# Theta and token mixing of the first three units as whole fp32 products, with their weights split afterwards

## The chip, the cores and the metric

One core of a Trainium2 chip runs one kernel with one launch. The metric is device time in microseconds (us). The engines are called here by their profile names or in words: PE (TensorE, products), PEld (its weight loads), DVE (VectorE), ACT (ScalarE), POOL (GpSimd) and SP (which issues every copy of this kernel). The kernel before takes 648.9 us, the median of three runs (648.49 to 651.3).

## What is computed

Three layers run one after another on 4 sequences of 768 tokens with 384 channels. The attention is a recurrence with a decay per channel; the second layer turns each channel by an angle, mixes over tokens with two 768x768 matrices and then over channels; the third is a gated layer. The change lies in the second layer.

```python
# attention, per head:  state = alpha_t * state + k_t v_t^T ;  y_t = q_t . state
theta = x @ w_theta
zr, zi = x * cos(theta), x * sin(theta)
y = einsum('ts,bsd->btd', w_tok_r, zr) + einsum('ts,bsd->btd', w_tok_i, zi)
u = x + y
x2 = u + maximum(u @ w_ch, 0)
h = maximum(x2 @ w_in, 0)
u3, v = h[..., :512], h[..., 512:]
v_s = einsum('ts,bsd->btd', w_spatial, layernorm(v)) + b_spatial
out = (u3 * v_s) @ w_out
```

The weights w_theta, w_tok_r, w_tok_i, w_ch, w_in and w_out arrive as 64-bit floats. The rest is fp32.

## The kernel before, in words

**Units.** A unit `u` is 128 tokens of one sequence. There are 24, six to a sequence (a "batch", `b`). For each unit the attention runs first (lines 442 to 556: two scans on DVE, `kh` and `qh`, scores `psa`, state `psu`, output `psy`). Then come theta and the mixing: a transposition `pst` (line 568), copies `xh` and `xT` of it, theta (`th_p`, lines 591 and 594), rounding and sine (`kk`, `r`, `z`), `z` times `x` (line 620), and the token mixing `tokmix` (line 652), which adds this unit's six products (three groups of 128 channels, real and imaginary) into five accumulators `acc` of its batch. After a batch's sixth unit the accumulators are added to `xT` (`evac`, line 666), one is cleared for the next batch (`acc_zero`, line 661), and the channel mixing `ch_p` (line 689) follows. The third layer (lines 763 to 870) runs after all units.

**Products in three.** A theta or mixing product is made of reduced fp32 (fp32r) operands. Each operand is held as a high part, which is the rounded value, and a low part, which is what the rounding left. High times high, high times low and low times high are added. For theta that is nine products of 384 columns a unit (six at line 591, three at line 594). For one mixing step it is six instructions, three of 512 and three of 256 columns. The attention products are whole fp32 instead: one instruction in the code, shown as two records in the trace.

**Weights.** A weight piece is 128 rows of 384 numbers. `conv` (line 370) issues ten or so steps for one: a copy of the 64-bit words into one of two buffers `raw` (line 313), `sgn` and `sign` on ACT (lines 319 and 341; for one piece in four the first is on DVE, line 321), `bits` and `join` on DVE (lines 329 and 336), `mag` on ACT (line 344), the product with the sign `mul` (line 349), the high part `high` on ACT (line 355, or 357 for theta) and the low part `low` (line 364, or 366 for theta). The first 30 pieces are three of w_theta, four for each unit of a batch from the two mixing matrices, and three of w_ch; they are all wanted while the first batch runs. GpSimd does `mul` of every third piece (`MULP`), `low` of two in four (`LOP`), and the low part of `z` (`z_l`, line 629) of the first six units (`ZLP`).

**Order.** A planner (`order` and `latest`, lines 86 and 195) lists all steps by due time, moved by a table of offsets per kind of step (`OFF`, and `OFF0`, `OFF3` for the first and last batch), and the instructions are issued in that list's order. Every engine works through its own instructions strictly in it. PSUM has three shared buffers (`psp`), beside the accumulators.

Of the kernel before, what the change touches and what calls it, by code (L numbers as in the profile page):

```python
# [218 lines left out]
def attention_mixer_kernel(  # L219
# [131 lines left out]
    def high(n):
        c = cvs[n]
        f = c["f"].rearrange("p (a b) -> p a b", a=c["a"])
        if c["scale"] is None:
            nc.scalar.copy(out=c["part"](0), in_=f)  # L355
        else:
            nc.scalar.activation(c["part"](0), f, AF.Identity, scale=c["scale"])

    def low(n):
        c = cvs[n]  # L360
        f = c["f"].rearrange("p (a b) -> p a b", a=c["a"])
# [1 line left out]
        if c["scale"] is None:
            c["eng"].tensor_tensor(out=c["part"](1), in0=f, in1=h, op=ALU.subtract)  # L364
        else:
            nc.vector.scalar_tensor_tensor(
                out=c["part"](1), in0=f, scalar=c["scale"], in1=h, op0=ALU.mult, op1=ALU.subtract
            )

    def conv(src, part, key, tiles=(), scale=None):  # L370
# [8 lines left out]
        if src.dtype == I64:  # L379
            k0 = step(OFF["raw"], "dma", 1.6, raw_f64, n, after=before, tiles=[raw, *tiles])  # L380
            raws.append(k0)
            k1 = step(OFF["sgn"], *(("act", 0.54) if n % 4 < SGA else ("dve*", 0.27)), sgn, n, after=[k0], tiles=[raw, sg])
            k2 = step(OFF["bits"], "dve*", 0.27, bits, n, after=[k0], tiles=[raw, cv])
            k2 = step(OFF["bits"], "dve*", 0.47, join, n, after=[k2], tiles=[raw, cv])
            k3 = step(OFF["sgn"], "act", 0.52, sign, n, after=[k1], tiles=[sg])
# [743 lines left out]
```

## Time and profile before

| | before |
|---|---|
| median of 3 runs | 648.9 us |
| the profiled execution | 648.46 us, of which its span in the trace is 646.7 us |
| PE busy | 600.4 us (93%) |
| DVE busy | 431.3 us (67%) |
| ACT busy | 283.4 us (44%) |
| POOL busy | 79.2 us (12%) |

PE is busy nearly all the time, so only two things can change the span: how much work PE has, and how long it stands idle or runs at the slower of its two clock levels. In the page's 40 slices the idle time lies in the first eight (0 to 130 us). DVE is busiest in just these slices, and so is POOL.

### The profile page before, as it was taken

To read this page: it belongs to the slowest core of one execution; us is meant where nothing else is said; L and a number is where in the kernel's file an instruction comes from. 1 tells how busy PE (TensorE), PEld (TensorE's weight loads), DVE (VectorE), ACT (ScalarE), POOL (GpSimd) and SP (SyncE) were. 2 spreads that over 40 slices of the span, in tenths; PEclk is the share of its full clock that TensorE was granted. 3 is DMA by queue.
4 is the path that set the end of the run, shared out by engine and by line. 5 is a ranking of instruction groups with operands and counts; after the bars stand their busy time and mean duration, and the time that the engine had idled before them with its cause. 6 is when DMAs were issued, how large, how long until landed. Compare 5 with 4: busy or idle time off the path is not lost.

```text
span 646.7 us, 13064 instructions
## 1 busy us (share of the span) xinstructions
PE 600.4 (93%) x5364; PEld 560.2 (87%) x5364; DVE 431.3 (67%) x779; ACT 283.4 (44%) x544; POOL 79.2 (12%) x78
## 2 busy tenths in 40 slices
PE   1476697999999999999999999999999999999997
PEld 1465586788888889988888999999999999999997
DVE  6978988799878787777867768684536533563331
ACT  3357677675234353332448744462423331333122
POOL 1023253241000000000001122220100010010000
PEclk9987999999999999999999999999999999999999
DMA  7766644542532243342224464320100010001002
GB/s 200 203 186 185 186 135 135 152 119 61 155 116 74 79 119 98 104 116 77 60 77 133 131 218 144 139 98 1 50 25 0 14 38 25 1 13 50 13 1 73
DMA packets 41147, 61.46 MB, mean 95 GB/s; under 512 B 4864, under 2 KB 30720, under 8 KB 40576
## 3 DMA queue, kind: packets, MB, share of 16 engines
q1 hardware_dynamic: 41088, 60.64, 31.6%
q8 instruction: 42, 0.69, 0.4%
q14 instruction: 17, 0.14, 0.1%
HBM read 47.94 MB, written 9.44 MB: 89 GB/s over the span
## 4 chain that ended last, share of the span: by engine, by line
PE 85%; DMA 5%; DVE 4%; ACT 3%; SPq 1%; issue 1%; POOL 0%; DVEq 0%; ACTq 0%; POOLq 0%
PE acc L652 22%; PE sp L833 15%; PE psv L776 8%; PE pu L818 8%; PE po L862 8%; PE psc L689 6%; PE psy L549 6%; PE th L591 4%; PE psa L482 3%; PE psu L515 2%; DMA raw<-in_w_theta 2%; PE th L594 2%; DMA raw<-in_w_tr 1%; PE psk L499 1%; DMA sd<-ss 1%; PE pst L568 1%
## 5 line engine op out<-in xcount | busy, mean ns | idle before, releaser
L652 PE MATMUL acc<-w,zs 128*128 128x512 f32 (+1 forms) x864 | 174.7, 347 | 0.0
L652 PEld LDWEIGHTS acc<-w,zs 128*128 128x128 f32 x864 | 135.0, 190 | 18.2 <-issue 0.2
L833 PE MATMUL sp<-w,vns 128*128 128x384 f32 x576 | 105.0, 336 | 0.0
L833 PEld LDWEIGHTS sp<-w,vns 128*128 128x128 f32 x576 | 99.9, 188 | 0.0
L849 ACT CAST gs<-t 128x384 fp32r<-128x384 f32 x32 | 16.3, 513 | 99.1 <-DVE t L843 94.4
L818 PE MATMUL pu<-xs,w 128*128 128x384 f32 x288 | 55.7, 337 | 0.0
L776 PE MATMUL psv<-w,xs 128*128 128x256 f32 x432 | 55.5, 283 | 0.0
L842 DVE TENSOR_TENSOR t<-sp,bsb 128x384 f32<-128x384 f32 x32 | 17.8, 557 | 55.5 <-PE sp L833 55.0
L776 PEld LDWEIGHTS psv<-w,xs 128*128 128x128 f32 x432 | 54.5, 191 | 0.2
L862 PE MATMUL po<-w,gs 128*128 128x384 f32 x288 | 53.0, 336 | 0.0
L818 PEld LDWEIGHTS pu<-xs,w 128*128 128x128 f32 x288 | 50.8, 188 | 0.0
L862 PEld LDWEIGHTS po<-w,gs 128*128 128x128 f32 x288 | 49.8, 188 | 0.0
L349 POOL TENSOR_TENSOR wf<-wf,sg 128x384 f32<-128x384 f32 x14 | 17.6, 1259 | 245.9 <-ACT wf L344 244.3
L549 PE MATMUL psy<-sd,qh 112*64 112x96 f32 x352 | 36.7, 262 | 11.8 <-DMA sd<-ss 5.1
L482 PE MATMUL psa<-qh,kh 48*64 48x64 f32 x768 | 30.2, 233 | 17.2 <-DVE kh L463 16.5
L482 PEld LDWEIGHTS psa<-qh,kh 48*64 48x64 f32 x768 | 26.8, 145 | 22.2 <-DVE kh L463 17.0
L689 PE MATMUL psc<-us,wch 128*128 128x256 f32 x324 | 43.3, 284 | 0.0
L689 PEld LDWEIGHTS psc<-us,wch 128*128 128x128 f32 x324 | 40.9, 190 | 0.9
L549 PEld LDWEIGHTS psy<-sd,qh 112*64 112x64 f32 x352 | 24.9, 143 | 17.0 <-issue 7.4
L364 POOL TENSOR_TENSOR w<-wf,w 128x384 fp32r<-128x384 f32 x24 | 28.7, 1198 | 68.8 <-ACT w L355 68.7
L549 PE MATMUL psy<-vd,am 128*64 128x96 f32 x384 | 36.7, 263 | 0.0
L455 DVE TENSOR_TENSOR_SCAN al<-al,heads 112x536 f32<-112x536 f32 x24 | 34.2, 1423 | 0.8
(83 smaller groups left out, 962.3 us busy)
## 6 DMA issues: line engine op xcount, KB each, us to landing
qk<-in_qka SPq DMA_DIRECT2D x24, 448.0 KB, 4.3
al<-in_qka SPq DMA_DIRECT2D x24, 234.5 KB, 3.0
vd<-in_vt SPq DMA_DIRECT2D x48, 96.0 KB, 2.5
raw<-in_w_tr SPq DMA_DIRECT2D x12, 384.0 KB, 4.0
raw<-in_w_ti SPq DMA_DIRECT2D x12, 384.0 KB, 3.7
x2d<-xT SPq DMA_DIRECT2D x12, 384.0 KB, 3.1
x<-x2d SPq DMA_DIRECT2D x4, 1152.0 KB, 5.2
out<-o SPq DMA_DIRECT2D x24, 192.0 KB, 1.9
```

The source lines that it names most:

```text
L364: c["eng"].tensor_tensor(out=c["part"](1), in0=f, in1=h, op=ALU.subtract)
L455: nc.vector.tensor_tensor_scan(out=line, data0=line, data1=one, initial=0.0, op0=ALU.mult, op1=ALU.add)
L482: nc.tensor.matmul(psa[o0:o0 + 64, a, c, :], kh[r0:r0 + D, a, c, :], qh[r0:r0 + D, a, c, :], start=True, stop=True,)
L549: nc.tensor.matmul(psy[64 * c:64 * c + 64, a, :], w[:, a, c, :], v[:, c, :, a, :], start=part == 0 or first, stop=part == 1,)
L591: nc.tensor.matmul(th, xh[:, 0, k], wth[:, pr, k], start=(k == 0 and pr == 0), stop=False)
L652: nc.tensor.matmul(acc[b, n][:, c0:c1], zs[:, pl, ri, m * 128:(m + 1) * 128], w[:, pr, t0:t1], start=first and n != 1, stop=last, skip_gro ...
L689: nc.tensor.matmul(ps, wch[:, pl, k, m * 128:(m + 1) * 128], us[:, pr, k], start=(n == 0), stop=(n == 3 * KD - 1),)
L776: nc.tensor.matmul(ps[:, c], xs2[:, pl, k, o:o + 128], w[:, pr, k], start=(n == 0), stop=(n == 3 * KD - 1),)
L818: nc.tensor.matmul(pu, win[f // 2][:, pl, (f % 2) * KD + k], xq[b, h][:, pr, k], start=(n == 0), stop=(n == 3 * KD - 1),)
L833: nc.tensor.matmul(sp[:, :TH], vns[b, s][:, pl, f * 128:(f + 1) * 128], wsp[s][:, pr, h], start=(n == 0), stop=(n == 3 * NS - 1),)
L842: nc.vector.tensor_tensor(out=t1, in0=s2.pop(("sp", b, f, h))[:, :TH], in1=bsb[0][:, t], op=ALU.add)
L862: nc.tensor.matmul(po, gs[b][:, pl, f, s * 128:(s + 1) * 128], wo[f // 2][:, pr, f % 2], start=(n == 0), stop=(n == 3 * KF - 1),)
```

## The change

For units 0 to 2 theta and the token mixing take the operands whole, in fp32: one product where there were three. `z` of these units is written once and has neither a high nor a low part; `xh` is not made. Their weights (w_theta, and the pieces of both matrices for the first three rows) are kept whole in four extra buffers `wf` out of the twelve of `w`; the high and low parts, which batches 1 to 3 still want, are made after the last product that reads the whole form (`users`, `held`). The scale of w_theta moves into `mag`. `LOP`, `MULP` and `ZLP` are set so that GpSimd gets no `low`, `mul` or `z_l` at all. All offset tables have new numbers, and there are two new ones, per unit in the batch order (`UNIT`, added in `at`) and per weight piece (`PIECE`, added in `conv`).

```diff
-LOP = 2
+LOP = 0
-MULP = 3
-ZLP = 6
+MULP = 99
+ZLP = 0
+FU = 3
...
     def mag(n):
-        nc.scalar.activation(cvs[n]["f"], cvs[n]["f"], AF.Abs)
+        nc.scalar.activation(cvs[n]["f"], cvs[n]["f"], AF.Abs, scale=cvs[n]["scale"])
...
     def mul(n):
         c = cvs[n]
         eng = nc.gpsimd if c["mulp"] else nc.vector
-        eng.tensor_tensor(out=c["f"], in0=c["f"], in1=c["sg"], op=ALU.mult)
+        f = c["f"]
+        if c["users"]:
+            a = c["a"]
+            f, sg = (x.rearrange("p (a b) -> p a b", a=a) for x in (f, c["sg"]))
+            eng.tensor_tensor(out=c["hold"](), in0=f, in1=sg, op=ALU.mult)
+            return
+        eng.tensor_tensor(out=f, in0=f, in1=c["sg"], op=ALU.mult)
+
+    def whole(n):
+        c = cvs[n]
+        return c["hold"]() if c["users"] else c["f"].rearrange("p (a b) -> p a b", a=c["a"])
...
+        nc.scalar.copy(out=cvs[n]["part"](0), in_=whole(n))
...
+        c["eng"].tensor_tensor(out=c["part"](1), in0=whole(n), in1=h, op=ALU.subtract)
...
-        k = step(OFF["high"], "act", 0.41, high, n, after=[k], tiles=[cv, *tiles])
+        k = step(early + OFF["high"], "act", 0.41, high, n, after=[k, *users], tiles=[*(held or [cv]), *tiles])
...
+    def f_tile(key):
+        if key not in wf:
+            wf[key] = wpool.tile([128, 2, S], F32, tag="w", name="wf", bufs=12)
+        return wf[key]
...
     def conv_tok(ri, s):
         src = (w_tr, w_ti)[ri]
         w = w_tile(wt, (ri, s), 1)
+        after = [("low", n) for n in sorted(late)] if (ri, s) == (1, NS - 1) else []
         for h in range(2):
             c = slice(h * TH, (h + 1) * TH)
+            more = {}
+            if s < FU:
+                late.add(len(cvs))
+                more = {
+                    "users": [("tokmix", s, m, ri) for m in range(KD)],
+                    "hold": lambda c=c: f_tile(s)[:, ri, None, c], "held": [("w", 12, ("f", s))],
+                }
...
+    def th_f(u):
+        th = st[u]["th"] = ps_tile([128, DM], "th")
+        for k in range(KD):
+            nc.tensor.matmul(th, xt_ap(u)[:, k], wth_whole()[:, k], start=(k == 0), stop=(k == KD - 1))
...
     def z_m(u):
         z, x = st[u]["z"], st[u]["x"]
-        nc.vector.tensor_tensor(out=z, in0=z, in1=x[:, None, :].to_broadcast([128, 2, DM]), op=ALU.mult)
+        out = z
+        if u < FU:
+            st[u]["zs"] = pb.tile([128, 2, 2, DM], F32, tag="zs", name="zf", bufs=3)
+            out = st[u]["zs"][:, 1]
+        nc.vector.tensor_tensor(out=out, in0=z, in1=x[:, None, :].to_broadcast([128, 2, DM]), op=ALU.mult)
...
-        w = wt[ri, i]
-        for pl, pr in ((0, 0), (0, 1), (1, 0)):
-            first = i == 0 and ri == 0 and pl == 0 and pr == 0
+        whole = u < FU
+        w = wf[i][:, ri, None] if whole else wt[ri, i]
+        for pl, pr in ((1, 0),) if whole else ((0, 0), (0, 1), (1, 0)):
+            first = i == 0 and ri == 0 and (whole or pl == 0 and pr == 0)
...
-            return step(OFF[name] + more.get(name, 0.0), eng, cost, fn, u, *args, after=after, tiles=tiles, by=by)
+            return step(OFF[name] + more.get(name, 0.0) + UNIT.get(str(u), 0.0), eng, cost, fn, u, *args, after=after, tiles=tiles, by=by)
```

What that does to the order is seen at three places. GpSimd, from its start, before; `sd` and `vd` are attention tiles that are cleared, `wf` and `w` a weight piece whole and split, `sg` its sign, `zs` the parts of `z`:

```order
L277 MEMSET sd_96 112x768
L280 MEMSET vd_98 128x768
L277 MEMSET sd_100 112x768
L280 MEMSET vd_102 128x768
L349 ISA
L349 TENSOR_TENSOR wf<-wf,sg 128x384
L364 TENSOR_TENSOR w<-wf,w 128x384
```

and now, the same stretch; the last row is a step of the third layer:

```order
L288 MEMSET sd_96 112x768
L291 MEMSET vd_98 128x768
L288 MEMSET sd_100 112x768
L291 MEMSET vd_102 128x768
L841 ISA
L841 TENSOR_TENSOR rs<-rs,mhalf 128x1 x24
```

All 46 products, low parts of weights and low parts of `z` that stood between the two are gone from it; they stand on DVE now, except the `z` parts of units 0 to 2, which are gone.

PE at the first token mixing, unit 0, before; each of the last two rows stands there three times, in turn, for the three parts:

```order
L568 MATMUL pst<-cst_sb,x 128x128 x3
L499 MATMUL psk<-cst_sb,kh 128x112 x4
L482 MATMUL psa<-qh,kh 64x64 x16
L652 MATMUL acc_109<-w,zs 128x256
L652 MATMUL acc_666<-w,zs 128x512
```

and now:

```order
L584 MATMUL psy<-sd_96,qh 64x96 x2
L584 MATMUL psy<-vd_98,am 64x96 x2
L697 MATMUL acc_109<-wf,zf 128x256
L697 MATMUL acc_533<-wf,zf 128x512
L697 MATMUL acc_549<-wf,zf 128x512
L697 MATMUL acc_550<-wf,zf 128x256
L550 MATMUL psu<-vn,kt 64x48
```

A mixing step is two instructions in place of six, and it stands ahead of the scores `psa` of unit 4 and not behind them.

DVE where batch 0 ends and batch 1's accumulator is cleared, before (`xT` receives the accumulators, `wch` is a piece of w_ch):

```order
L336 SCALAR_TENSOR_TENSOR wf<-raw,wf 128x384
L666 TENSOR_TENSOR xT<-acc_773,xT 128x512
L666 TENSOR_TENSOR xT<-acc_109,xT 128x256
L349 TENSOR_TENSOR wf<-wf,sg 128x384 x2
L666 TENSOR_TENSOR xT<-acc_109,xT 128x256
L666 TENSOR_TENSOR xT<-acc_666,xT 128x512
L364 TENSOR_TENSOR wch<-wf,wch 128x384
L329 TENSOR_SCALAR wf<-raw 128x384
L661 MEMSET acc_1743 128x512
```

and now:

```order
L711 TENSOR_TENSOR xT<-acc_658,xT 128x512
L711 TENSOR_TENSOR xT<-acc_109,xT 128x256
L348 SCALAR_TENSOR_TENSOR wf<-raw,wf 128x384
L379 TENSOR_TENSOR wch<-wf,wch 128x384
L711 TENSOR_TENSOR xT<-acc_109,xT 128x256
L711 TENSOR_TENSOR xT<-acc_533,xT 128x512
L367 TENSOR_TENSOR wf<-wf,sg 128x384
L706 MEMSET acc_1843 128x512
```

The clearing is DVE's instruction 222 before and 267 now.

## Rows read from the trace of the kernel before

**Rows 1.** Busy time by stretch: length; busy us (instructions) by engine; clock; DMA.
```profile
0.00:13.00 13.00, 0.28 (x5) 0.28 (x6) 6.78 (x17) 3.86 (x7) 2.97 (x8) 1.00 0.68 186
13.00:60.00 47.00, 27.94 (x412) 23.86 (x411) 39.16 (x75) 26.03 (x53) 9.25 (x7) 0.88 0.73 197
60.00:126.00 66.00, 55.07 (x549) 48.27 (x550) 56.89 (x100) 44.77 (x91) 25.04 (x16) 0.93 0.53 153
126.00:646.70 520.70, 517.15 (x4406) 487.81 (x4404) 328.53 (x590) 208.72 (x396) 41.94 (x48) 1.00 0.25 76
```

**Rows 2.** The same view, one stretch of PE at its lower clock.
```profile
55.80:62.50 6.70, 5.58 (x44) 4.73 (x45) 5.27 (x12) 4.97 (x10) 3.42 (x3) 0.50 0.69 211
```

**Rows 3.** Waits of DVE, 7 to 126 us: total us, times, longest.
```profile
DVE sg L321 <- DMA raw<-in_w_tr: 6.0, 3, 4.5
...
DVE xh L581 <- ACT xT L577: 3.0, 3, 1.3
```

**Rows 4.** Single lines of DVE, 7 to 126 us: duration ns min/median/max.
```profile
L455 DVE TENSOR_TENSOR_SCAN al<-al,heads x9: 1274/1276/2487, 9.6 to 107.5; 112x536 f32<-112x536 f32 x9
...
L470 DVE TENSOR_TENSOR qh<-qk,al x9: 679/691/2322, 11.4 to 113.1; 112x512 f32<-112x512 f32 x9
...
L329 DVE TENSOR_SCALAR wf<-raw x25: 329/354/1435, 7.2 to 123.9; 128x384 uint32<-128x384 uint32 x25
```

**Rows 5.** Groups of DVE, 7 to 126 us: busy us, mean ns of one, idle before.
```profile
L455 DVE TENSOR_TENSOR_SCAN al<-al,heads 112x536 f32<-112x536 f32 x9 | 14.6, 1625 | 0.3
...
L329 DVE TENSOR_SCALAR wf<-raw 128x384 uint32<-128x384 uint32 x25 | 10.8, 433 | 8.2 <-DMA raw<-in_w_theta 4.9 <-DMA raw<-in_w_ti 2.9 <-DMA raw<-in_w_tr 0.2
L349 DVE TENSOR_TENSOR wf<-wf,sg 128x384 f32<-128x384 f32 x16 | 8.9, 555 | 1.4 <-ACT wf L344 1.4
L470 DVE TENSOR_TENSOR qh<-qk,al 112x512 f32<-112x512 f32 x9 | 8.6, 958 | 1.0 <-PE psy L549 1.0
...
L620 DVE TENSOR_TENSOR z<-z,x 128x768 f32<-128x768 f32 x5 | 4.9, 972 | 0.6 <-ACT z L614 0.6
```

**Rows 6.** Instructions of DVE in order, 90 to 96 us: start, duration.
```profile
90.51 0.68 DVE L489 TENSOR_TENSOR am<-psa,cst_sb 128x512 f32<-128x512 f32 x1
91.11 0.35 DVE L537 TENSOR_TENSOR tmp<-psu,ss 112x192 f32<-112x192 f32 x1
...
91.89 1.27 DVE L451 TENSOR_TENSOR_SCAN rt<-al,heads 112x536 f32<-112x536 f32 x1
...
93.44 2.49 DVE L455 TENSOR_TENSOR_SCAN al<-al,heads 112x536 f32<-112x536 f32 x1
```

**Rows 7.** The same stretch on POOL.
```profile
91.92 2.88 POOL L629 TENSOR_TENSOR zs<-z,zs 128x768 fp32r<-128x768 f32 x1 [0.37 <-DVE ss L524]
```

**Rows 8.** The chain that ended last: start us, us, what.
```profile
7.23 0.65 ACT sg L319
...
157.25 1.08 PE psa L482 x32
...
170.49 1.48 PE psy L549 x32
171.97 0.53 PE psk L499 x4
...
177.81 0.60 PE psu L515 x26
...
182.89 1.05 PE acc L652 x6
```

**Rows 9.** PE in order: `psy` near 195 us.
```profile
195.36 0.33 PE L549 MATMUL psy<-sd,qh 112*64 112x96 f32 x4
195.53 0.34 PE L549 MATMUL psy<-vd,am 128*64 128x96 f32 x4
```

**Rows 10.** PE in order where the first mixing of unit 6 begins.
```profile
146.69 0.49 PE L568 MATMUL pst<-cst_sb,x 128*128 128x128 f32 x3
146.94 1.29 PE L652 MATMUL acc<-w,zs 128*128 128x256 f32 x6
```

More of the change, by code (lines that the diff above doesn't have):

```diff
@@ L43 @@
 OFF = {
[6 rows of a table removed]
-    "sgn": -23.49, "mag": 39.17, "mul": -72.53, "high": -59.59, "low": 17.5, "v": -1.84, "vr": 121.16, "vb": 138.25,
-    "vw": -48.53, "vm": 45.12, "vh": -80.17, "vl": 72.49, "g_u": -21.79, "g_r": -32.74, "g_s": -40.03, "g_m": -104.87,
-    "g_h": -88.37, "g_l": 5.15, "o_p": -6.46, "o_e": 26.76, "x2h": 78.95, "x2l": 23.69, "x2": -32.84,
[6 rows of a table added]
+    "bits": 19.52, "sgn": -39.0, "mag": 43.2, "mul": -77.37, "high": -58.7, "low": 7.1, "v": 9.91, "vr": 13.15,
+    "vb": -3.08, "vw": 17.45, "vm": -5.55, "vh": -54.65, "vl": 17.18, "g_u": -9.94, "g_r": -6.45, "g_s": -45.14,
+    "g_m": -139.46, "g_h": -63.43, "g_l": -44.96, "o_p": 13.88, "o_e": -31.29, "x2h": 130.7, "x2l": 57.91,
+    "x2": -170.04,
 }
@@ L302, in attention_mixer_kernel @@
     conv_done = {}
+    conv_whole = {}
     raws = []
@@ L348, in mul, with conv @@
         eng = nc.gpsimd if c["mulp"] else nc.vector
-        eng.tensor_tensor(out=c["f"], in0=c["f"], in1=c["sg"], op=ALU.mult)
-    def high(n):
[L352 to L357, printed above, removed]
+        f = c["f"]
[8 more added lines that the diff above has]
+        return c["hold"]() if c["users"] else c["f"].rearrange("p (a b) -> p a b", a=c["a"])
+    def high(n):
+        nc.scalar.copy(out=cvs[n]["part"](0), in_=whole(n))
     def low(n):
         c = cvs[n]
-        f = c["f"].rearrange("p (a b) -> p a b", a=c["a"])
         h = c["part"](0).bitcast(F32)
[L363 to L370, printed above, removed]
+        c["eng"].tensor_tensor(out=c["part"](1), in0=whole(n), in1=h, op=ALU.subtract)
+    def conv(src, part, key, tiles=(), scale=1.0, users=(), hold=None, held=(), wait=()):
         n = len(cvs)
-        c = {"src": src, "a": src.shape[1], "part": part, "scale": scale}
+        early = PIECE.get(str(n), 0.0)
+        c = {"src": src, "a": src.shape[1], "part": part, "scale": scale, "users": users, "hold": hold}
         cvs.append(c)
-        pool = scale is None and n % 4 < LOP
+        pool = n % 4 < LOP
         c["eng"] = nc.gpsimd if pool else nc.vector
@@ L379, in conv @@
         if src.dtype == I64:
-            k0 = step(OFF["raw"], "dma", 1.6, raw_f64, n, after=before, tiles=[raw, *tiles])
+            k0 = step(early + OFF["raw"], "dma", 1.6, raw_f64, n, after=before + list(wait), tiles=[raw, *(held or tiles)])
             raws.append(k0)
[L382 to L385, printed above, removed]
+            k1 = step(early + OFF["sgn"], *(("act", 0.54) if n % 4 < SGA else ("dve*", 0.27)), sgn, n, after=[k0], tiles=[raw, sg])
+            k2 = step(early + OFF["bits"], "dve*", 0.27, bits, n, after=[k0], tiles=[raw, cv])
+            k2 = step(early + OFF["bits"], "dve*", 0.47, join, n, after=[k2], tiles=[raw, cv])
+            k3 = step(early + OFF["sgn"], "act", 0.52, sign, n, after=[k1], tiles=[sg])
             c["mulp"] = n % MULP == MULP - 1
-            k2 = step(OFF["mag"], "act", 0.42, mag, n, after=[k2], tiles=[cv])
-            k = step(OFF["mul"], *(("pool*", 0.96) if c["mulp"] else ("dve*", 0.47)), mul, n, after=[k3, k2], tiles=[sg, cv])
+            k2 = step(early + OFF["mag"], "act", 0.42, mag, n, after=[k2], tiles=[cv])
+            k = step(early + OFF["mul"], *(("pool*", 0.96) if c["mulp"] else ("dve*", 0.47)), mul, n, after=[k3, k2], tiles=[sg, cv, *held])
+            conv_whole.setdefault(key, []).append(k)
         else:
-            k = step(OFF["raw"], "dma", 0.8, raw_f32, n, after=before, tiles=[cv, *tiles])
+            k = step(early + OFF["raw"], "dma", 0.8, raw_f32, n, after=before, tiles=[cv, *tiles])
             raws.append(k)
-        k = step(OFF["high"], "act", 0.41, high, n, after=[k], tiles=[cv, *tiles])
-        k = step(OFF["low"], *(("pool*", 0.96) if pool else ("dve*", 0.47)), low, n, after=[k], tiles=[cv, *tiles])
+        k = step(early + OFF["high"], "act", 0.41, high, n, after=[k, *users], tiles=[*(held or [cv]), *tiles])
+        k = step(early + OFF["low"], *(("pool*", 0.96) if pool else ("dve*", 0.47)), low, n, after=[k], tiles=[*(held or [cv]), *tiles])
         conv_done.setdefault(key, []).append(k)
@@ L404, in w_tile, with wth_whole @@
         return part
+    late = set()
+    wf = {}
+    def f_tile(key):
+        if key not in wf:
+            wf[key] = wpool.tile([128, 2, S], F32, tag="w", name="wf", bufs=12)
+        return wf[key]
+    def wth_whole():
+        return f_tile("th").rearrange("p a b -> p (a b)")[:, :KD * DM].rearrange("p (k f) -> p k f", k=KD)
     def conv_tok(ri, s):
@@ L878, in attention_mixer_kernel @@
     step(0.0, "dma", 0.6, load_cst)
-    conv_small(w_theta, wth, "wth", scale=INV_2PI)
+    conv_small(w_theta, wth, "wth", more=lambda k: {
+        "scale": INV_2PI, "users": [("th_f", u) for u in range(FU)],
+        "hold": lambda: wth_whole()[:, k:k + 1], "held": [("w", 12, ("f", "th"))],
+    })
     for s in range(NS):
```

42 lines of the change are left out of this document (26 added, 16 removed), and 36 rows, old and new, of tables (OFF, OFF0, OFF3, PIECE).

## The prediction

> **What bounds the kernel now.** I began with the busy time by stretch [rows 1]. From 126 us on PE is busy 517.2 of 520.7 us at the full clock: there the span is PE's own work. Before that it is not. From 13 to 126 us PE works 83.0 of 113 us, and part of that at the lower of its two levels (granted clock 0.50, 1.2 GHz, [rows 2]). DVE is busy 96.1 of the same 113 us, the most of all engines. Its list in that time holds the attention of eight or nine units and the splitting of 30 weight pieces, so what PE lacks is mostly what DVE has not yet made.
>
> Next, the 17 us that DVE stands idle there. The waits say what for: raw weight copies (6.0 us at line 321, 2.9 and 0.2 at line 329; its 4.9 for w_theta are the start), the copies of the transposed unit on ACT (3.0), the magnitude of a piece on ACT (1.4), PE (1.0) and smaller ones [rows 3, 5].
>
> Last, DVE's busy time is itself longer than its work. A scan of line 455 takes 1.28 us as a rule and 2.49 at worst, a `qh` 0.69 and 2.32, a `bits` 0.35 and 1.44 [rows 4]. The order of time shows when: the scan of 2.49 us stands beside GpSimd's low part of `z`, which began at 91.92 and took 2.88 us [rows 6, 7]. The scan ends (95.9) soon after that low part does (94.8). By means against medians [rows 4, 5] these lines lost 9 x 0.35 + 9 x 0.27 + 25 x 0.08 = 7.6 us; with a few others I put it at 8.5. So GpSimd's help costs DVE part of what it saves.
>
> **A ledger at one point.** To compare the two orders I take one instruction that both have: the first mixing product of unit 6, which opens batch 1. Before, it starts at 146.9 us [rows 10], with 646.7 - 146.9 = 499.8 us of span behind it. It waits for the clearing of the accumulator on DVE, and DVE's part begins with the first raw copy at 7.2 us [rows 8]. So in the new order it starts at 7.2 + (DVE's work ahead of the clearing) + (DVE's waits w), if DVE is what binds.
>
> DVE's work is counted from the order and priced by the distance of neighbours' starts, which is some 0.08 below the duration: `am` 0.68, next start 0.60 later [rows 6]. So 0.27 for the 0.35 instructions, 0.47 for the 0.55 ones, 0.87 for `z`, 0.60 for `kh`, `qh`, `am` [rows 4 to 6], and 2.74 for a unit's two scans with the reciprocal (1.55 to the second scan's start and 1.19 for it undisturbed).
>
> Before: 9 scans 24.7, 27 of 0.60 16.2, 33 state steps 8.9, `bits` and `join` (30 and 29) 21.7, 20 `mul` 9.4, 16 `low` 7.5, 7 signs 1.9, 7 `r` and 8 `xl` 7.1, 7 `z` and one low part 7.0, the first batch's end 2.7: **107.0 us**.
> After: 11 scans 30.1, 33 of 0.60 19.8, 41 state steps 11.1, `bits` and `join` (29 each) 21.5, 29 `mul` 13.6, 28 `low` 13.2, 7 signs 1.9, 8 `r` and 6 `xl` 6.6, 8 `z` and 5 low parts 11.3, end 2.7: **131.7 us**.
>
> Of the 24.7 us more, some 13 come from GpSimd (12 `low`, 9 `mul`, 4 low parts of `z`); the rest is attention of units 9 and 10, brought forward. The two `z` parts and the two `xl` of the first units that vanish are already off.
>
> **What PE has done by then.** The same forward move lies in PE's order: attention of units 9 and 10 stands ahead of the point now, 2 x (1.08 + 0.53 + 0.60 + 1.48), theta of unit 8, 1.59 (nine products of 384 columns at the 1.05 / 2304 us of a mixing step's), and one transposition, 0.25 (146.94 - 146.69) [rows 8, 10]: 9.2 us. So 499.8 - 9.2 = 490.6 us remain behind the point. The span is 7.2 + 131.7 + w + 490.6 = **629.5 + w**, and it is even with before at w = 17.2.
>
> **The whole products.** The trace has none of this shape. From below: an attention output is two records a product, and four records (two products of 96 columns, for the two halves of the output) start 0.17 us apart from the next four [rows 9]. If the halves followed each other, a column costs 0.87 ns, if they run at once, 1.74. The scores give 1.08 / 16 = 0.068 us for 64 columns [rows 8], 1.05 or 2.1 ns the same two ways. A mixing step of three reduced products costs 1.05 for 2304 columns, 0.46 ns each [rows 8]. So a whole mixing step of 768 columns costs 0.67 to 1.61 us in place of 1.05, and I take 1.33 (1.74, the psy row, as its stationary operand fills all rows). A whole theta, 1152 columns, is 2.0 in place of 1.59. For 18 steps and three thetas that is +5.0 and +1.2, 6.2 us more (-8.6 to +12.6). The Trainium skill, "FP8 and Floating Point Precision", section "TensorE Precision Notes", speaks against this part of the change: true fp32 takes four passes. The trace shows two records a product, not four; but four passes at 0.46 ns a column would be 1.84 ns, near the row I took, and the added PE work would be 8.1 us, under the same cover.
>
> These 6.2 us all lie ahead of the point, where PE's list is 101.9 us long (86.5 before, plus 9.2, plus 6.2) in the 152 us or so until the point. Even with the 12.7 us before its first product (five records by 13 us, [rows 1]) and 15 more that I allow for the lower clock (half of the 27.9 us that PE is busy from 13 to 60), it has cover. If that cover is gone, they cost their 6.2.
>
> **Waits.** With GpSimd silent the 8.5 us of stretched instructions go: no row shows a DVE instruction of double length without a GpSimd one beside it. Of the idle time, the raw waits of 9.1 us should shrink: with two raw buffers a copy starts when the piece two before it is split, and there are 131.7 / 29 = 4.5 us of DVE work to a piece where there were 107.0 / 30 = 3.6. I take 4. The ACT replies (3.0, 1.4, 0.6 and smaller, 5.4) grow with the longer stretch, but the first three units need no `xl`: 5. PE replies 1.5 become 2 (early scores at the lower clock). Small gaps, 2. So w = 13, between 5 (raw waits hidden, ACT halved) and 26 (waits per us of DVE work as before: 17.0 on 96.1 - 8.5 = 87.6 us of work, times 131.7).
>
> Two waits are added. `high` of the late pieces stands on ACT behind the mixing of its unit; behind it in ACT's queue are signs and magnitudes that DVE waits for. The copy of the last two mixing pieces waits for all late `low`s; these stand some 24 us of DVE work earlier, so it should be met, and SP's queue behind it (attention inputs, state moves) is not held. Both are in the upper half of w.
>
> **Sum.** 629.5 + 13 = 642.5 us of span, 1.8 around it (648.46 - 646.7), and 0.4 by which that execution lies under the median: **644.7 us**.
>
> **Rivals.**
> 1. *The waits go with the work (slower).* In one order a queue that runs full waits as often per instruction as before: DVE answers to two raw buffers and to ACT, and now has no helper to run while it waits. The price is w = 21 to 26: 652.7 to 657.7 us. It decides from w = 20.4 on (652.1). For it: DVE stands 7.8 of the 47 us from 13 to 60 already [rows 1], when PE is far from full. Against it: 4.5 of the 17 us are one single raw copy [rows 3], no rate.
> 2. *PE is late at first (no change).* Whole theta and mixing stand early, where PE has the lower clock and a price of twice 1.33; `r` and `am` of units 1 to 3 then wait for PE, and the late `high` on ACT for the mixing. That adds 4 to 6 us to w: 648.7 to 650.7. For it: 17.2 us of PE work at full clock stand ahead of the first mixing, DVE has made its `z` by 7.2 + 32.7 = 39.9 us, and from 12.7 to 39.9 PE at 1.2 GHz gets through 13.6. Against it: DVE has weight pieces to split meanwhile.
> 3. *The stretching is not GpSimd's.* Then 8.5 us stay in w: 653.2. The pair of rows 6 and 7 speaks against it.
> That the change does not do what it says is excluded by GpSimd's order.
>
> **Chances.** About 0.5% is what a measurement of this kernel tells from no change: 645.7 to 652.1 us, w from 14.0 to 20.4. The forecast (w 8 to 14, faster) gets 0.47, and w under 8 another 0.03; rival 2 and w of 14 to 20 get 0.27; rivals 1 and 3 get 0.19 and 0.04. So faster 0.50, same 0.27, slower 0.23. The range leaves out w under 5 and over 24: 636.5 to 655.7.
>
> **What would show it.** In the new profile POOL is empty until the third layer, no DVE scan exceeds 1.3 us, and DVE is over 90% busy from 13 to 150 us. Unit 6's first mixing starts near 152 us, later than before, with PE saturated behind it and 490 us to go. A whole mixing step takes 1.2 to 1.45 us at full clock. Were the start at 160 us or later, w was wrong; were PE to wait behind it, the ledger's last term was.

## The result, and the profile after

The changed kernel takes 641.9 us (median of 4 runs, 640.4 to 642.5); the kernel before, on the same chip, 649.5 (648.5 to 651.3). The ratio is 0.988, 95% interval 0.985 to 0.991. The forecast was 644.7 us. The profiled execution took 641.73 us, its span is 640.0.

The page of the changed kernel, span, busy time and the slices of three engines:

```profile
span 640.0 us, 12937 instructions
PE 604.1 (94%) x5319; PEld 550.5 (86%) x5319; DVE 431.1 (67%) x819; ACT 281.2 (44%) x538; POOL 16.6 (3%) x32
...
PE   1789988889999999999999999999999999999997
...
DVE  5999999979756867678795687784516541664050
...
POOL 1000000000000000000000000100100110010000
```

PE is busy 3.7 us longer than before (600.4) and the span is 6.7 us shorter, so PE stood idle 10.4 us less. Where, the busy time by stretch says (columns as in [rows 1]):

```profile
0.00:13.00 13.00, 0.00 (x0) 0.00 (x0) 6.16 (x16) 3.63 (x6) 2.96 (x8) 1.00 0.69 188
13.00:60.00 47.00, 40.21 (x511) 29.71 (x511) 43.38 (x84) 26.54 (x54) 0.00 (x0) 0.96 0.69 201
60.00:126.00 66.00, 57.81 (x586) 43.63 (x581) 65.16 (x133) 49.28 (x99) 0.00 (x0) 0.95 0.58 168
126.00:640.00 514.00, 506.12 (x4232) 477.20 (x4230) 316.42 (x589) 201.76 (x381) 13.67 (x24) 1.00 0.24 75
```

Against [rows 1]: from 13 to 60 us PE is busy 40.2 us where it was 27.9, at a granted clock of 0.96 where it was 0.88. DVE is busy 108.5 of the 113 us from 13 to 126 (96.1 before), and POOL not at all. What DVE still waits for, 7 to 150 us (columns as in [rows 3]):

```profile
DVE wf L341 <- DMA raw<-in_w_theta: 5.5, 1, 5.5
DVE wf L341 <- DMA raw<-in_w_ti: 2.0, 2, 1.7
DVE wf L341 <- DMA raw<-in_w_ch: 1.9, 1, 1.9
DVE wf L365 <- ACT wf L356: 0.7, 2, 0.6
DVE kh L498 <- DMA qk<-in_qka: 0.7, 1, 0.7
DVE ss L559 <- DMA sd<-ss: 0.5, 1, 0.5
DVE wf L341 <- DMA raw<-in_w_tr: 0.5, 1, 0.5
DVE sg L333 <- DMA raw<-in_w_tr: 0.5, 1, 0.5
DVE tmp L572 <- PE psu L550: 0.2, 1, 0.2
```

The first row is the start (the wait ends at 7.86 us with the first piece). The rest is 7.0 us: raw copies 4.9, other copies 1.2, ACT 0.7, PE 0.2. Groups of DVE in the same stretch (columns as in [rows 5]):

```profile
L348 DVE SCALAR_TENSOR_TENSOR wf<-raw,wf 128x384 uint32<-128x384 uint32 x29 | 16.0, 552 | 0.1
L490 DVE TENSOR_TENSOR_SCAN al<-al,heads 112x536 f32<-112x536 f32 x11 | 14.0, 1275 | 0.4
...
L524 DVE TENSOR_TENSOR am<-psa,cst_sb 128x512 f32<-128x512 f32 x11 | 7.4, 677 | 0.0
L559 DVE TENSOR_TENSOR ss<-tmp,rt 112x192 f32<-112x192 f32 x20 | 7.1, 353 | 0.5 <-DMA sd<-ss 0.5
L572 DVE TENSOR_TENSOR tmp<-psu,ss 112x192 f32<-112x192 f32 x19 | 6.7, 352 | 0.3 <-PE psu L550 0.2
```

The scan has a mean of 1275 ns where it was 1625 [rows 5]: it is not stretched any more. Last, PE in order (start, duration), at full clock, with the whole products (`wf`, `zf`, `xT`), and where unit 6 begins to be mixed:

```profile
47.81 2.75 PE L697 MATMUL acc<-wf,zf 128*128 128x256 f32 x8
50.40 0.55 PE L534 MATMUL psk<-cst_sb,kh 112*128 112x112 f32 x4
...
52.65 2.20 PE L634 MATMUL th<-wf,xT 128*128 128x384 f32 x6 [0.63 <-ACT kt L538]
54.69 1.45 PE L697 MATMUL acc<-wf,zf 128*128 128x512 f32 x4
...
148.08 1.08 PE L697 MATMUL acc<-w,zs 128*128 128x256 f32 x5 [0.65 <-DVE acc L706]
```

Two steps are eight records and take 50.40 - 47.81 = 2.59 us, 1.30 each; a theta takes 54.69 - 52.65 = 2.04.

### The profile page after: what moved, and what is told of

Its sections match the earlier page's. It is cut to its first block, busy times and chain, and to the rows that moved or that the text cites. A ratio compares the mean times of both kernels' runs of the same rounds, so it can differ in the third digit from the quotient of the medians.

```text
span 640.0 us, 12937 instructions
## 1 busy us (share of the span) xinstructions
PE 604.1 (94%) x5319; PEld 550.5 (86%) x5319; DVE 431.1 (67%) x819; ACT 281.2 (44%) x538; POOL 16.6 (3%) x32
## 4 chain that ended last, share of the span: by engine, by line
PE 73%; DVE 14%; DMA 8%; ACT 2%; issue 1%; SPq 1%; POOL 0%; DVEq 0%; ACTq 0%; POOLq 0%
PE sp L878 16%; PE acc L697 15%; PE pu L863 8%; PE po L907 8%; PE psv L821 8%; PE psc L734 5%; PE psy L584 3%; PE th L626 2%; DMA raw<-in_w_ti 2%; PE psa L517 2%; DMA sd<-ss 2%; PE psu L550 1%; DVE rt L486 1%; DVE w L379 1%; PE th L629 1%
## 5 line engine op out<-in xcount | busy, mean ns | idle before, releaser
L697 PE MATMUL acc<-w,zs 128*128 128x512 f32 (+1 forms) x756 | 152.4, 347 | 0.7 <-DVE acc L706 0.6
L697 PEld LDWEIGHTS acc<-w,zs 128*128 128x128 f32 x756 | 118.1, 190 | 16.7 <-DVE acc L706 0.9
L898 DVE TENSOR_TENSOR gs<-t,gs 128x384 fp32r<-128x384 f32 x32 | 17.5, 555 | 43.3 <-ACT gs L894 42.9
L584 PE MATMUL psy<-sd,qh 112*64 112x96 f32 x352 | 35.4, 254 | 2.8 <-DMA sd<-ss 2.1
L584 PE MATMUL psy<-vd,am 128*64 128x96 f32 x384 | 34.9, 253 | 0.0
L871 ACT ACTIVATE ur<-pu 128x384 f32<-128x384 f32 x32 | 15.6, 489 | 36.0 <-DVE t L888 21.7
L490 DVE TENSOR_TENSOR_SCAN al<-al,heads 112x536 f32<-112x536 f32 x24 | 30.6, 1275 | 0.8
```

What stands on the lines that cost most here:

```text
L490: nc.vector.tensor_tensor_scan(out=line, data0=line, data1=one, initial=0.0, op0=ALU.mult, op1=ALU.add)
L584: nc.tensor.matmul(psy[64 * c:64 * c + 64, a, :], w[:, a, c, :], v[:, c, :, a, :], start=part == 0 or first, stop=part == 1,)
L697: nc.tensor.matmul(acc[b, n][:, c0:c1], zs[:, pl, ri, m * 128:(m + 1) * 128], w[:, pr, t0:t1], start=first and n != 1, stop=last, skip_gro ...
L898: nc.vector.tensor_tensor(out=gs[b][:, 1, f, t], in0=s2.pop(("t1", b, f, h)), in1=gs[b][:, 0, f, t].bitcast(F32), op=ALU.subtract)
```

## The experiments

All kernels but `fu0` and `old_tables` keep the order of instructions of the kernel they are made from; `early_raw` and `old_early` move four copies in it. Beside these runs, on three chips, the kernel before took 649.4 to 649.9 us, some tenths of a us from the 649.5 above. One ledger, the prediction's own, reads them all. Of every profiled execution I took the start of DVE's first piece, the start C of the clearing of the second accumulator, and the span. DVE's work W ahead of the clearing is counted from the order with the prediction's prices (in `dve_plus` the added work at its measured price, see there). The stretch X is, for each group of DVE from 7 to 150 us, its mean less its mean in a run without early GpSimd work, times its number. What is left is DVE's waiting: C + 0.5 - first piece - W - X.

| kernel | median us | first piece | C | W | X | waiting | span - C | span |
|---|---|---|---|---|---|---|---|---|
| before | 649.5 | 7.23 | 145.83 | 107.0 | 12.0 | 20.1 | 500.9 | 646.7 |
| changed | 641.9 | 7.86 | 147.54 | 131.7 | 0 | 8.5 | 492.5 | 640.0 |
| dve_plus | 651.3 | 7.82 | 154.80 | 143.0 | 0 | 4.5 | 492.9 | 647.7 |
| act_plus | 646.1 | 7.64 | 152.19 | 131.7 | 0 | 13.4 | 492.7 | 644.9 |
| pe_plus | 658.3 | 7.82 | 164.50 | 131.7 | 0 | 25.5 | 492.3 | 656.8 |
| pe_small | 647.9 | 7.13 | 151.99 | 131.7 | 0 | 13.7 | 491.8 | 643.8 |
| sgn_act | 641.9 | 7.51 | 145.44 | 129.8 | 0 | 8.6 | 492.9 | 638.3 |
| pool_noise | 645.9 | 7.34 | 151.68 | 131.7 | 6.5 | 6.6 | 493.3 | 645.0 |
| pool_back | 645.6 | 7.38 | 150.79 | 119.2 | 13.3 | 11.4 | 492.1 | 642.9 |
| old_dve | 650.2 | 7.34 | 147.50 | 122.5 | 0 | 18.2 | 501.5 | 649.0 |
| fu0 | 651.5 | 7.44 | 148.51 | 129.5 | 0 | 12.1 | 500.0 | 648.5 |
| old_tables | 654.6 | 8.01 | 154.56 | 131.4 | 0 | 15.7 | 497.7 | 652.3 |
| early_raw | 639.1 | 4.26 | 143.04 | 131.7 | 0 | 7.6 | 493.4 | 636.4 |
| old_early | 646.3 | 4.15 | 143.06 | 107.0 | 12.5 | 19.9 | 500.7 | 643.7 |

With the changed kernel's order, span - C stays between 491.8 and 493.4 us in all nine rows while C moves by 21 us. So all that happens ahead of the clearing passes into the time, and nothing is given back later.

### Which engine binds: more work for one at a time

`dve_plus`, in the changed kernel:

```diff
-        nc.vector.tensor_scalar(
-            out=fb, in0=c["raw"][:, :, 0], ...
-        )
+        for _ in range(2 if n < 30 else 1):
+            nc.vector.tensor_scalar(
+                out=fb, in0=c["raw"][:, :, 0], ...
+            )
```

> The changed kernel with the same order, in which DVE does the first word operation (bits) of each of the first 30 weight pieces twice: 29 of them ahead of the clearing of the second accumulator, 0.27 us each by the distance of starts, so 7.8 us more DVE work there and nothing else. Theory (DVE's work sets the moment at which batch 1 begins, one for one, and PE's own work sets all behind it): 7.8 us more, less what the raw waits of DVE (4.9 us in the changed kernel) absorb, since the copies then have longer: 645 to 650 us from 641.9. Rival (DVE is busy but no longer what binds; PE's or ACT's replies set the pace): 641 to 643.5.

Measured 651.3 us (ratio to before 1.003, 1.001 to 1.004), 9.4 over the changed kernel and above the range; C moved by 7.3 in the profiled execution, the fastest of ten. The price of 0.27 us was too low. The repeated operation writes the same tile, and the next instruction behind the pair starts 0.66 us after it, where one alone takes 0.27:

```profile
132.13 0.75 DVE L342 TENSOR_SCALAR wf<-raw 128x384 uint32<-128x384 uint32 x2
132.79 0.69 DVE L499 TENSOR_TENSOR kh<-qk,rt 112x512 f32<-112x512 f32 x1
```

So a repeat costs 0.39 us, and 29 of them are 11.3 us more DVE work, not 7.8. DVE's raw waits, the first apart, fell from 4.9 us to this one row, so they did absorb a part, as the expectation had it:

```profile
DVE wf L342 <- DMA raw<-in_w_tr: 0.2, 1, 0.2
```

Of a us of DVE work 0.65 came through by C (7.3 of 11.3) and 0.8 by the medians (9.4 of 11.3).

`act_plus`:

```diff
-        nc.scalar.activation(cvs[n]["f"], cvs[n]["f"], AF.Abs, scale=cvs[n]["scale"])
+        for _ in range(2 if n < 30 and cvs[n]["scale"] == 1.0 else 1):
+            nc.scalar.activation(cvs[n]["f"], cvs[n]["f"], AF.Abs, scale=cvs[n]["scale"])
```

> The changed kernel with the same order, in which ACT takes the magnitude (mag) of each of the first 30 pieces but the three of w_theta twice, 26 or 27 more instructions of 0.52 us, 14 us more ACT work ahead of batch 1, with DVE's mul waiting for each of them. Theory (ACT has room: 75.8 us busy of the 113 from 13 to 126): 0 to 3 us more, 642 to 645. Rival (ACT's replies are what the late start of batch 1 hangs on): half of the 14 or more, 649 to 656.

Measured 646.1 (0.995, 0.993 to 0.996), 4.2 more, 0.3 for each us of ACT: between the two. ACT has room, but not all of it where DVE waits for an answer. Waits of DVE, 7 to 160 us:

```profile
DVE wf L368 <- ACT wf L357: 2.3, 6, 0.7
DVE wf L366 <- ACT wf L357: 1.6, 4, 0.8
```

`pe_plus`, and `pe_small` with the doubling for `u == 1` alone:

```diff
-        for pl, pr in ((1, 0),) if whole else ((0, 0), (0, 1), (1, 0)):
-            first = i == 0 and ri == 0 and (whole or pl == 0 and pr == 0)
+        for n2, (pl, pr) in enumerate(((1, 0), (1, 0)) if whole else ((0, 0), (0, 1), (1, 0))):
+            first = i == 0 and ri == 0 and n2 == 0
```

> The changed kernel with the same order, in which each whole mixing product of units 0 to 2 is issued and added twice, so the mixing of these units counts double in the output. That is 18 steps of 1.29 us, 23.2 us more PE work ahead of batch 1, more than three times what the whole products themselves added (6.2). Theory (PE has cover there; it stands idle or at its lower clock for 46 us by the start of batch 1): 0 to 6 us more, 642 to 648. Rival (the cover is spent, since PE is 85 to 88% busy from 13 to 126 us): 15 to 23 us more, 657 to 665; then the 6.2 us are in the changed kernel's time as well.

> The changed kernel with the same order, in which only the six whole mixing steps of unit 1 are issued and added twice (so unit 1 counts double in the output): 7.7 us more PE work ahead of batch 1, a little more than the 6.2 that the whole products added. Theory of the prediction (work of this size has cover on PE): 0 to 2 us more, 642 to 644. Rival (PE is as near to binding as DVE; 17 of 23.2 us came through when all 18 steps were doubled, 0.73 a us): 5 to 6 us more, 647 to 648.

Measured 658.3 (1.013, 1.012 to 1.015), 16.4 more for 23.2 us of PE work, and 647.9 (0.997, 0.996 to 0.999), 6.0 more for 7.7. The rival holds both times: a us of PE work ahead of batch 1 costs 0.7 to 0.8 us. Where, DVE's waits of `pe_small` from 60 to 126 us say, and the busy time by stretch, first two stretches of the changed kernel:

```profile
60.00:75.00 15.00, 14.33 (x135) 9.76 (x129) 14.83 (x32) 9.86 (x22) 0.00 (x0) 1.00 0.58 165
75.00:92.00 17.00, 15.20 (x166) 10.00 (x167) 16.54 (x34) 12.51 (x26) 0.00 (x0) 1.00 0.68 198
```

then of `pe_small`, and its wait:

```profile
60.00:75.00 15.00, 15.00 (x80) 8.79 (x78) 10.48 (x21) 5.24 (x11) 0.00 (x0) 1.00 0.35 102
75.00:92.00 17.00, 16.33 (x222) 12.34 (x220) 13.99 (x27) 11.51 (x23) 0.00 (x0) 1.00 0.59 169
```

```profile
DVE tmp L572 <- PE psu L550: 6.7, 2, 4.9
```

In the changed kernel PE is busy 29.5 of these 32 us, and DVE too (31.4). The doubled steps stand ahead of a unit's `psu` in PE's queue; `tmp` waits for it, and DVE's queue behind `tmp`. From 64.80 to 75.23 us PE works through 32 records of mixing in a row, and DVE's longer wait ends behind them:

```profile
77.46 0.36 DVE L572 TENSOR_TENSOR tmp<-psu,ss 112x192 f32<-112x192 f32 x1 [4.95 <-PE psu L550]
```

The cover of 46 us that my expectation took from the whole stretch lay elsewhere: 13 us before the first product, the rest in other stretches, where PE waits for DVE or runs at its lower clock.

`sgn_act`, DVE's seven sign operations to ACT:

```diff
-        if n % 4 < SGA:
+        if n % 4 < SGA or n < 30:
```

> The changed kernel with the same order, in which the sign operation of every piece runs on ACT; seven of DVE's, 0.27 us each, leave its list ahead of batch 1 (1.9 us) and ACT gets seven of 0.65. Theory (DVE's work counts one for one, ACT has room): 1 to 2 us less, 640 to 641. Rival (DVE's work is not what binds, or ACT's longer list answers DVE later): 641.5 to 643.5.

Measured 641.9 (0.988, 0.987 to 0.990): nothing, as the rival had it. The profiled execution, the fastest of four, has C 2.1 us earlier, but the median of the runs does not show it. By the two slopes above, 1.9 us less on DVE and 7 x 0.65 = 4.5 more on ACT are about -1.2 to -1.6 and +1.4, which is nothing.

### What GpSimd's silence is worth

`pool_back` puts GpSimd's early work back on it, at the places where it now stands on DVE; `old_dve` does the reverse in the kernel before:

```diff
-        eng = nc.gpsimd if c["mulp"] else nc.vector
+        eng = nc.gpsimd if n < 30 and n % 3 == 2 else nc.vector
...
-        c["eng"].tensor_tensor(out=c["part"](1), ...
+        eng = nc.gpsimd if 3 <= n < 30 and n % 4 < 2 else nc.vector
+        eng.tensor_tensor(out=c["part"](1), ...
...
-        eng = nc.gpsimd if u < ZLP else nc.vector
+        eng = nc.gpsimd if u < 6 else nc.vector
```

> The changed kernel with the same order, in which GpSimd does again what it did before: mul of every third of the first 30 pieces, low of two in four, the low part of z for units 3 to 5. 12.5 us of DVE's work leave its list ahead of the clearing (131.7 to 119.2). Theory of the prediction (GpSimd stretches DVE's instructions by some 8.5 us, DVE's work counts one for one): scans over 1.3 us come back, and the time moves by -12.5 + 8.5 and the replies of the slow GpSimd instructions (1.2 and 2.9 us each, 26 of them) that DVE and ACT wait for: 638 to 646 us. Rival 1 (the stretching is not GpSimd's): no long scans, 631 to 636. Rival 2 (the silence of GpSimd is what the change lives from): 648 to 652, as before.

> The kernel before with its own order, in which all that GpSimd did for weights and for z stands at the same places on DVE. DVE's list ahead of the clearing grows from 107.0 to 122.5 us, PE's stays. Theory (one for one, the 8.5 us of stretched instructions go, the rest of the idle time stays as it was): 649.4 + 15.5 - 8.5 = 656; if the raw waits (9 us) are absorbed by the longer list, 648. Rival (GpSimd's silence alone makes the gain, whole products and tables nothing): 640 to 644. In either case no scan over 1.3 us, unless the stretching is not GpSimd's.

`pool_back` measured 645.6 (0.994, 0.992 to 0.996), 3.7 more; `old_dve` 650.2 (1.001, 0.999 to 1.003), no change. The latter lies between its theory's two figures, 656 and 648: the stretch that went was 12.0 us and not 8.5, and the raw waits were not absorbed (9.3 us, 9.1 before). Groups of DVE in `pool_back`, 7 to 150 us:

```profile
L348 DVE SCALAR_TENSOR_TENSOR wf<-raw,wf 128x384 uint32<-128x384 uint32 x29 | 17.6, 606 | 0.1
L491 DVE TENSOR_TENSOR_SCAN al<-al,heads 112x536 f32<-112x536 f32 x11 | 16.0, 1453 | 0.4
...
L341 DVE TENSOR_SCALAR wf<-raw 128x384 uint32<-128x384 uint32 x29 | 13.7, 474 | 8.2 <-DMA raw<-in_w_theta 5.0 <-DMA raw<-in_w_ch 1.6 <-POOL w L380 0.9
...
L560 DVE TENSOR_TENSOR ss<-tmp,rt 112x192 f32<-112x192 f32 x20 | 11.1, 555 | 0.6 <-DMA sd<-ss 0.5
```

and the scan in `old_dve`:

```profile
L455 DVE TENSOR_TENSOR_SCAN al<-al,heads 112x536 f32<-112x536 f32 x9 | 11.5, 1275 | 0.3
```

The long instructions come and go with GpSimd. In the changed order its help takes 12.5 us off DVE and gives 13.3 back as stretch, and the waiting grows by 2.9. In the old order DVE's 15.5 us more are paid by 12.0 us of stretch and 1.9 of waiting that go. So the silence alone is worth nothing in the old order and 3.7 us in the new one.

`pool_noise` measures the stretch by itself:

```diff
+    spare = const.tile([128, 320], F32, name="spare")
     def mul(n):
         c = cvs[n]
+        if n < 30:
+            nc.gpsimd.tensor_tensor(out=spare, in0=c["sg"][:, :320], in1=c["sg"][:, :320], op=ALU.mult)
```

> The changed kernel with the same order and nothing taken from DVE, in which GpSimd multiplies 320 columns of the sign tile of each of the first 30 pieces into a spare tile that nobody reads: 30 instructions of about 1.05 us by the size (1.2 for 384 columns), 31 us of GpSimd work in the first 150 us. Theory (it is GpSimd's mere running that stretches DVE's instructions; with 37 us of it, the trace with GpSimd put back shows 13.3 us of stretch): 11 us of stretch, scans and bits of double length, 648 to 654 us. Rival (the long instructions are not GpSimd's doing, or come only where both work on one tile): no stretch, 641 to 643.

Measured 645.9 (0.994, 0.991 to 0.996), 4.0 more: over the rival's range and under the theory's. The 30 instructions took 36.2 us of GpSimd, and the stretch was 6.5 us, not 11; the longest scan took 1.6 us and not double, and `bits` stayed at 355 ns. So the cause holds, and the size was off. GpSimd's own instructions are of very unequal length too, from 0.72 to 4.00 us for the same work, so part of the 36.2 us is waiting and not work; 30 times the shortest would be 22 us, an estimate. Two of them:

```profile
105.43 0.72 POOL L363 TENSOR_TENSOR spare<-sg 128x320 f32<-128x320 f32 x1 [7.18 <-ACT sg L353]
108.88 3.27 POOL L363 TENSOR_TENSOR spare<-sg 128x320 f32<-128x320 f32 x1 [2.73 <-ACT sg L353]
```

The same groups of DVE as above:

```profile
L348 DVE SCALAR_TENSOR_TENSOR wf<-raw,wf 128x384 uint32<-128x384 uint32 x29 | 17.6, 606 | 0.1
...
L563 DVE TENSOR_TENSOR ss<-tmp,rt 112x192 f32<-112x192 f32 x20 | 8.5, 426 | 0.4 <-DMA sd<-ss 0.4
...
L528 DVE TENSOR_TENSOR am<-psa,cst_sb 128x512 f32<-128x512 f32 x11 | 7.4, 672 | 0.0
L576 DVE TENSOR_TENSOR tmp<-psu,ss 112x192 f32<-112x192 f32 x19 | 6.6, 346 | 0.1
```

`ss` and `join` (L348) are longer than in the changed kernel (353 and 552), `am` and `tmp` are not (677 and 352). The first two read two operands from SBUF, the others one from SBUF and one from PSUM (`psa`, `psu`). The Trainium skill, "SBUF — State Buffer", section "SBUF: two separate sides", states such a rule: a DVE instruction in a mode that takes two ports, or with two SBUF inputs against a GpSimd one that reads SBUF, and the GpSimd instruction take turns at a shared port pair, and the loser waits for the whole instruction of the other. The rows of `ss`, `join`, `am` and `tmp`, and the unequal lengths on GpSimd, agree with it. `bits` reads one operand only and was stretched in `pool_back` (474 ns) and not in `pool_noise` (355, against 353 in the changed kernel); whether it runs in such a mode, no run here shows.

### Whole products or tables

`fu0` sets `FU = 0` in the changed kernel; `old_tables` gives it the `OFF`, `OFF0` and `OFF3` of the kernel before and empties the two new tables:

```diff
-FU = 3
+FU = 0
```

```diff
-UNIT = {...}
-PIECE = {...}
+UNIT = {}
+PIECE = {}
```

> The changed kernel, with its tables and a silent GpSimd, without whole products: theta and mixing of units 0 to 2 from split weights again, put in order anew by the planner. By its order DVE has 129.5 us ahead of the clearing and PE 87.4 of 584.0, so the span is 7.2 + 129.5 + w + 496.6 = 633.3 + w. Theory (whole products matter by letting DVE put off 15 lows and drop three xl, so that it answers PE sooner; without them the waits are as before, w near 17 to 24): 652 to 659 us. Rival (whole products give nothing, tables and silence all; w near 9 as in the changed kernel): 644.

> The changed kernel, whole products and silent GpSimd, with the offset tables of the kernel before and none per unit or piece, put in order anew. By its order DVE has 131.4 us ahead of the clearing and PE 94.7 of 590.8: span 634.7 + w. Theory (the order that the tables give is what keeps DVE fed; with the old ones w is 17 to 24): 653 to 660 us. Rival (whole products and silence do it by themselves, w near 9): 645 to 646.

`fu0` measured 651.5 (1.003, 1.001 to 1.006), `old_tables` 654.6 (1.008, 1.005 to 1.011). Each half alone is no faster than before. By the expectations' own sums w is 15.2 us in `fu0` (648.5 - 633.3), under the range of 17 to 24, and 17.6 in `old_tables` (652.3 - 634.7), inside it. But not all of it is waiting ahead of the clearing: that was 12.1 and 15.7 us. In `fu0` 3.9 us are missing behind the clearing: 500.0 us where the order promised 496.1 (496.6 less the 0.5 between clearing and mixing). By stretch, 13 to 60 us, `fu0` first:

```profile
13.00:60.00 47.00, 33.76 (x469) 28.93 (x470) 44.62 (x88) 26.07 (x53) 0.00 (x0) 0.89 0.67 188
```

```profile
13.00:60.00 47.00, 32.93 (x453) 25.41 (x454) 41.12 (x80) 22.23 (x43) 0.00 (x0) 0.93 0.78 208
```

In both PE is busy 33 to 34 us until 60, against 40.2 with both halves and 27.9 with none. This shows that the two belong together, and no more: the tables belong to `FU = 3`, and what whole or split products would give with tables of their own stays open.

### The first copy

The wait of 5.5 us at the start stands in front of a chain that binds. In the changed kernel the queue of copies (SP) begins so:

```profile
2.17 1.34 SPq L477 DMA_DIRECT2D vd<-in_vt  x2
3.56 0.59 SPq L325 DMA_DIRECT2D raw<-in_w_theta  x1
```

Its first entry waits for GpSimd's clearing of `vd` (its last ends at 3.5 us, the one of unit 0 at 2.15). `early_raw` moves the four `vd` copies behind the second raw copy, and `old_early` does so in the kernel before:

```diff
-        for key in order(latest(steps, due)):
+        keys = order(latest(steps, due))
+        late_vt = [("load_vt", 0), ("load_vt", 1)]
+        keys = [k for k in keys if k not in late_vt]
+        n = keys.index(("raw_f64", 1)) + 1
+        for key in keys[:n] + late_vt + keys[n:]:
```

> The changed kernel, in which the four copies of vd for units 0 and 1 stand behind the second raw copy in the queue of copies and not ahead of the first one. In the changed kernel the queue waits until 2.17 us for GpSimd's clearing of vd and then spends 1.34 us on its two issues, so that the first raw copy is issued at 3.56, and DVE stands idle for it until 7.86. Theory (DVE's chain binds from its first piece on, one for one): the raw copy is issued up to 2.7 us earlier and the time falls by 1.5 to 2.7 us, 639 to 640.5. Rival (the copies come no earlier, since what they wait for is the start of the transfers, or the gain is lost in later waits): 641 to 643.

> The kernel before with the same move of the four vd copies, its order otherwise kept. Theory (there too DVE's chain binds from the first piece, but 20 us of waits stand in it that can take up a shift): 0.5 to 2.7 us less than before, 646.5 to 649. Rival (the gain of the move is lost in the waits): as before, 649 to 650.

`early_raw` measured 639.1 us (638.1 to 639.7; ratio to before 0.984, 0.982 to 0.985); its slowest run is below the fastest of the changed kernel. `old_early` measured 646.3 (0.995, 0.993 to 0.997), 3.6 less than before; the 20 us of waiting in the old order did not take it up (19.9 us). SP and DVE's first piece in `early_raw`:

```profile
0.73 0.40 SPq L325 DMA_DIRECT2D raw<-in_w_theta  x1
```

```profile
4.26 0.36 DVE L341 TENSOR_SCALAR wf<-raw 128x384 uint32<-128x384 uint32 x1 [1.91 <-DMA raw<-in_w_theta]
```

The first piece comes 3.6 us sooner and the span is 3.6 us shorter, one for one; by the medians the gain is 2.8 us. This kernel beats both.

## Why the prediction was right, and where not

- **What bounds.** Right as far as it went: the clearing follows DVE's list, one for one where the whole list shifts (`early_raw`), to 0.65 to 0.8 where work is added to it (`dve_plus`, the raw waits take up a part), and behind it PE's own work stands (span - C constant). It named DVE alone; PE binds as much there (0.7 to 0.8).
- **The ledger.** Predicted 7.2 + 131.7 + w + 490.6 = 629.5 + w. Measured: first piece at 7.9, first mixing of unit 6 at 148.1 (predicted near 152), 491.9 us behind it. So w is 640.0 - 629.5 = 10.5 by the prediction's own sum, of which 0.7 is the later first piece and 1.3 the last term. The waiting proper is 8.5, where 13 was forecast. There is some luck in how near the time came (641.9 us, forecast 644.7): the 4.5 us too many of waiting met 2.0 us too few in the two other terms. The lower end of the range was added up 0.2 us too low (629.5 + 5 + 2.2 is 636.7).
- **The step that was mis-sized** is w. Raw waits were 4.9 (taken as 4), ACT 0.7 (taken as 5), PE 0.2 (taken as 2), the rest 2.7 (taken as 2). I scaled the ACT replies with the length of the stretch. In the new order DVE hardly waits for a reply (0.7 us here, 2.1 in `early_raw`), and against the [rows 3] list the waits for `xT` are absent. That this is due to the `xh` and the `z` parts that are gone from the first units is not shown: `fu0` keeps these steps and has no wait for `xT` either, and each half of the change alone leaves some 4 us of ACT replies (4.3 in `fu0`, 4.0 in `old_tables`). Why they go with both stays open.
- **Stretch.** Forecast 8.5 us, from 7 to 126 us. By the means of `old_dve` it was 8.8 there, and 12.0 until 150 us: I left out the part from 126 us to the clearing, where `ss`, `sg` and `z` are stretched. Afterwards it is 0. That the silence of GpSimd would pay it back was right (`pool_back`), but the sum of stretch and added work is near nothing, so it isn't where the gain comes from. Rival 3 is out.
- **Where the gain is.** Between the first two rows of the ledger: W up 24.7, stretch down 12.0, waiting down 11.6, the part behind the clearing down 8.4, the first piece 0.6 later: 24.7 - 12.0 - 11.6 - 8.4 + 0.6 = -6.7, the difference of the spans.
- **The whole products.** 1.33 a mixing step and 2.0 a theta were forecast, 1.30 and 2.04 came. That their 6.2 us have cover was right by the row of DVE's waits for PE (0.2 us; no run takes just this work off PE), but for a wrong reason: I compared 101.9 us of PE work with 152 us of time. The cover is local and was used up; the next 7.7 us cost 6.0. The Trainium skill, "FP8 and Floating Point Precision", section "TensorE Precision Notes", has four passes for true fp32; by the estimate made from that, 1.84 ns a column, it is near the 1.69 measured (1.30 / 768), though the trace shows two records a product.
- **Rival 1** (w 21 to 26) fell, since the waits did not go with the work. **Rival 2**'s mechanism, DVE waiting for PE, did not come, but it was nearer than I gave it: `pe_small` is just that. Its slower clock did, by the durations of the products, but too early to matter. Groups of PE from 13 to 27 us, then from 28 to 37:

```profile
L584 PE MATMUL psy<-vd,am 128*64 128x96 f32 x16 | 2.7, 381 | 0.0
```

```profile
L584 PE MATMUL psy<-vd,am 128*64 128x96 f32 x16 | 1.5, 248 | 0.0
```

The same 16 records take 2.7 us and then 1.5. The first record of the granted clock in the trace stands at 27.8 us and is of 1.00, the higher level. The first whole theta begins at 30.4 us and the first whole mixing at 44.05; only the theta at 39.65 falls into a slow stretch (granted clock 0.50):

```profile
38.00:41.40 3.40, 3.40 (x27) 2.57 (x23) 3.33 (x6) 2.48 (x5) 0.00 (x0) 0.50 0.55 163
```

Behind that first record the clock stands at its lower level for 10.2 us until 126 us, where in the kernel before it was 20.5.

- **The two added waits** did not bite. DVE waited 0.7 us for ACT in all, and until 150 us no wait of the raw copies names a `low`.

## What to carry to other kernels

Where two engines feed each other in strict order, cover has to be read stretch by stretch: PE's work ahead of batch 1 was 46 us shorter than the time it had, and still 7.7 us more work cost 6.0. Give each engine in turn a known amount of work more; the three slopes (here 0.65 to 0.8 for DVE, 0.7 to 0.8 for PE, 0.3 for ACT) tell what binds, and that moving 1.9 us from DVE to ACT will not show. Read the amount from the trace of that run: the repeats in `dve_plus` cost 0.39 us each and not 0.27, and with the wrong price DVE seemed to bind one for one. And look first at the head of the chain that binds: one entry in a queue that waited for a buffer to be cleared cost 3 us for nothing.

## What the hardware showed that I had not expected

In the changed order GpSimd's help to DVE was worth nothing net: 12.5 us of work taken over, 13.3 us of DVE instructions stretched. How much it stretches is not a matter of GpSimd's busy time alone: from 7 to 150 us 33 us of it gave 13.3 us in `pool_back`, 36 us gave 6.5 in `pool_noise`, where GpSimd's own instructions took from 0.72 to 4.00 us for the same work. `am` and `tmp`, with an operand in PSUM, showed no stretch.

The view of the granted clock says nothing ahead of the trace's first clock record. From 13 to 27.8 us it shows 1.00, while 16 `psy` records there took 2.7 us and later 1.5; the first record stands at 27.8 us (35.3 in the kernel before), and time without a record is shown as 1.00. So the durations of like products tell more there than that view, and by them the mean clocks of the stretches that begin at 13 us, here and in [rows 1], are too high.
